# Attention followed by a gated expert layer: the fourth batch's first tiles turned by transposing transfers

## The chip, the cores and the metric

The kernel runs on one core of a Trainium2 chip. The metric is the device time of one execution in microseconds (us); less is better. Five engines run their own instruction streams in order and meet by semaphores: TensorE (PE in the profile, with its weight loads shown apart as PEld), VectorE (DVE), ScalarE (ACT), GpSimd (POOL) and SyncE (SP, which here only issues transfers). SBUF is the working memory of 128 partitions, PSUM the memory that TensorE writes to.

## The reference

All arithmetic is float32. Four batches, eight heads, 576 positions, head size 64:

```python
scores = q @ k^T / 8 + bias[h, i, j]      # bias: a small network of log1p(|i-j|) / log1p(max(i,1))
attn   = softmax(scores, axis=-1)         # exp(s - max) / (sum + 1e-9)
o      = attn @ v                         # (4, 8, 576, 64)
x      = o.transpose(0, 2, 1, 3).reshape(4 * 576, 512)
out    = ((x @ w_a) * (x @ w_b)) @ w_out  # w_a, w_b: 512 x 1536, w_out: 1536 x 512
```

## The kernel before

**Tiles.** Heads are taken in pairs (four pairs a batch). A unit is a batch, a pair and a half `c`: for `c = 0` the positions 0 to 255 of both heads, in four tiles of 128 rows of scores (`A0, B0, A1, B1`; A and B are the heads), for `c = 1` the positions 256 to 575 in five tiles (`A2, B2, A3, B3` and `T`, the last 64 rows of both heads). All `c = 0` units of the four batches come first (16 tiles a batch, tiles 0 to 63), then all `c = 1` units (20 tiles a batch, tiles 64 to 143). `N0 = 16`, `NF = 12` is the first unit of the fourth batch, `NP = 4`.

**One tile.** `qk` (L452) multiplies queries and keys into a PSUM pair `qk` (two banks, 288 keys in each); there is one such pair, so the scores of the next tile wait until VectorE has read those of this one. `soft1` (L489): VectorE adds the bias tile and takes the row minimum (L496, `p<-qk,bias`, minimum `mn`), ScalarE makes the exponential and its sum (L501). `soft2` (L540), one tile later: GpSimd and VectorE make the reciprocal `rc` (L544, L545), and then one of two ways is taken.

- Tiles 0 to 63: GpSimd scales the tile (L550), TensorE turns it in five 128-column pieces into a PSUM pair `tp` (`turn`, L562), ScalarE copies it to SBUF. In the fourth batch that copy is rounded to 16 bits (L578) and VectorE subtracts it from the PSUM tile for the rest (L579), so that `pt` holds high and low halves.
- Tiles 64 to 143, `split_turn` (L525): GpSimd writes the scaled tile rounded to 16 bits into the first half of a source buffer `ph` (L530), VectorE the rest into the second half in two instructions of 64 and 512 columns (L532), and SP issues one transposing transfer of `ph` into `pt` (L538). There are two `ph` buffers.

`pv` (L585) multiplies the turned tile with the values; in the fourth batch's first units it takes 15 products of both heads (30 matmuls), in `c = 1` units 14 (28 matmuls). The result goes as 16-bit high and low halves to `x`, the input of the expert layer.

**The second batch's scores** (tiles 16 to 31) are plain float32 products over 64 rows: head A's queries and keys stand on partitions 0 to 63, head B's on 64 to 127, and both matmuls of a tile (one for each half of the keys) read the same 64 partitions. The first batch's tiles are taken in pairs (`qk_pair`, L474): there the matmuls of a pair alternate between the two halves of the partitions, into two PSUM pairs.

**The expert layer** (`moe_block`, L684) for 256 rows: 24 steps of 12 matmuls (L698, `ab`), then 12 steps of 6 matmuls of the second product (L747, `o`). `merge` (L774) interleaves its steps with the steps of attention by fixed shares, and TensorE's order is this program order (`manual_schedule`, L796); the order on the other engines is planned when the kernel is built. Each block belongs to a batch and half whose attention is done. After the last attention step TensorE works through the rest of the expert layer alone.

**Bias.** The bias of rows 256 to 575 is made while the fourth batch's first tiles run: 20 units, each of four rectified rows (L143 on VectorE, L147 on ScalarE; `nact` of the four are on ScalarE), 32-column matmuls into PSUM (L153), copies (L169, L172) and a write to DRAM. One set of four `h` tiles is there.

**Order around the change.** In `attn_steps` (L621) step `n` runs `soft1(n)`, the preparation of units that begin soon, `qk(n + 1)`, `pv` of a unit that ended, `turn(n - 2)` and `soft2(n - 1)`; bias tiles are loaded two tiles ahead. At step 65 the pool of `pt` is closed and opened anew for the `c = 1` shapes (L667).

Of the kernel before, what the change touches and what calls it, by code (L numbers as in the profile page):

```python
# [8 lines left out]
F32 = mybir.dt.float32  # L9
# [43 lines left out]
def attention_moe(ctx, tc, q0d, q1d, kd, vd, idn, wp, wa, wb, wo, lsw, lg, rl, out):  # L53
# [10 lines left out]
    xt, cpool, epool, xpool = [], [None], [None], [None]  # L64
# [304 lines left out]
    def load_unit(u):  # L369
        b, hp, c = UNITS[u]  # L370
        n = TOK + TAIL * c
        if u < 2 * NP:
            rk = epool[0].tile([128, S], F32, tag="rkf", name="rkf", bufs=NP) if u < NP else \
                att.tile([128, S], F32, tag="ks", name="rkf", bufs=2)
            rq = epool[0].tile([128, TOK], F32, tag="rqf", name="rqf", bufs=NP) if u < NP else \
                att.tile([128, TOK], F32, tag="qs", name="rqf", bufs=2)
# [148 lines left out]
    def split_turn(n, p, rc):  # L525
        u, t = TILES[n]
        if t == "A2":
            st["pt", u] = cpool[0].tile([128, 9, 640], F16, tag="pt", name="pt", bufs=2)
        ph = cpool[0].tile([128, 2 * S], F16, tag="ph", name="ph", bufs=2)
# [7 lines left out]
        o = {"A2": 0, "A3": 128, "T": 256, "B2": 384, "B3": 512}[t]  # L537
        nc.sync.dma_start_transpose(out=st["pt", u][:, :, o:o + 128], in_=ph)  # L538

    def soft2(n):  # L540
# [5 lines left out]
        if UNITS[u][2]:  # L546
            split_turn(n, p, rc)
            return
# [7 lines left out]
    def turn(n, pool):  # L556
# [13 lines left out]
        if u < NF:  # L570
            if t == "A0":
                st["pt", u] = cpool[0].tile([128, 5, 512], F32, tag="pt", name="ptw", bufs=2)
            nc.scalar.copy(st["pt", u][:, :, o:o + 128], tp)
            return
        if t == "A0":
            st["pt", u] = cpool[0].tile([128, 10, 512], F16, tag="pt", name="pt", bufs=2)
        dst = st["pt", u][:, :, o:o + 128]
        nc.scalar.copy(dst[:, 0:5], tp)  # L578
        nc.vector.tensor_tensor(out=dst[:, 5:10], in0=tp, in1=dst[:, 0:5], op=ALU.subtract)  # L579
# [41 lines left out]
    def attn_steps():  # L621
        vgen = [None]
        for n in range(NT + 4):
# [11 lines left out]
            for ahead, un in ((a, TILES[n + a][0]) for a in (6, 4, 3, 1) if n + a < NT and FIRST[TILES[n + a][0]] == n + a):  # L635
# [11 lines left out]
                else:  # L647
# [20 lines left out]
            if n >= 2 and n - 2 < B * N0:  # L668
# [6 lines left out]
            elif N0 + 3 <= n < B * N0 + 3 and TILES[n - 3][0] != TILES[n - 2][0]:  # L675
# [123 lines left out]
    LEADS = [3] + [4] * 3 + [8] * 4  # L799
# [98 lines left out]
    n2, n3 = steps(2)[1], 2 * ((ends[3] - ends[2]) * 2 // 3)  # L898
# [4 lines left out]
    with tc.tile_pool(name="bg2", bufs=1, reuse_waits="tile") as bg:  # L903
# [71 lines left out]
```

## Time and profile before

| | us |
|---|---|
| median of three runs | 784.29 (778.23 to 787.6) |
| the profiled execution | 783.58 |
| its span, first to last instruction | 781.7 |
| TensorE busy | 724.0 (93%) |
| VectorE busy | 508.7 (65%) |
| ScalarE busy | 454.3 (58%) |
| GpSimd busy | 328.4 (42%) |
| mean granted TensorE clock | 0.985 |

A row of the profile names a line of the kernel, an engine, an operation and its tiles; "idle before" is the time in which the engine waited ahead of it, with what ended the wait. Matmuls are pipelined and their ends are modelled, so a busy TensorE is not one at its peak. The stages, by the start of the bias addition (L496) of their first tile: first batch to about 84 us, second to 159, third to 237, fourth to 337, the `c = 1` tiles to 650, and the expert layer alone to the end.

### The profile page before, as it was taken

The page shows a single profiled execution, that of the slowest core. Times are in us where ns is not written, and L with a number is a line of the kernel's source. Part 1 is how long each engine was busy: PE and PEld are TensorE (multiplying, and loading weights), DVE is VectorE, ACT ScalarE, POOL GpSimd, SP SyncE. Part 2 cuts the span into 40 slices and gives each one's busy share as a digit, 9 for nine tenths or more (in the row PEclk, how much of TensorE's full clock was granted, in tenths as well). Part 3 has the DMA queues.
Part 4 walks back from the last instruction along what each step waited for, and adds up shares of the span by engine and source line. Part 5 has one row for each costly group of instructions (what it writes and reads, how often), then busy time and mean ns, then how long its engine had stood idle before and what let it go on. Part 6 is the DMA issues. An engine that isn't in the chain of part 4 may idle for free.

```text
span 781.7 us, 15679 instructions
## 1 busy us (share of the span) xinstructions
PE 724.0 (93%) x5539; PEld 561.1 (72%) x5539; DVE 508.7 (65%) x1219; ACT 454.3 (58%) x1022; POOL 328.4 (42%) x493
## 2 busy tenths in 40 slices
PE   7778899999899999997888998998899999999998
PEld 1245566678777766786766777887787788888886
DVE  7677688679976788747878788877786762110100
ACT  6878787878866777744555455555554552421310
POOL 3347677856762233313444344534442453320200
PEclk9989999999999999999999999999999999999999
DMA  8998665688735555429988998999999863100001
GB/s 258 316 348 290 209 203 180 198 262 254 246 105 155 150 170 164 134 93 216 214 200 201 234 224 192 235 227 202 176 230 221 179 143 87 49 1 28 2 14 41
DMA packets 147699, 137.73 MB, mean 176 GB/s; under 512 B 101284, under 2 KB 105636, under 8 KB 147620
## 3 DMA queue, kind: packets, MB, share of 16 engines
q1 hardware_dynamic: 140464, 120.95, 58.9%
q10 hardware_dynamic: 5876, 10.93, 4.7%
q0 software_dynamic: 1280, 4.84, 1.8%
q8 instruction: 44, 0.72, 0.4%
q14 instruction: 35, 0.29, 0.1%
HBM read 95.91 MB, written 17.18 MB: 145 GB/s over the span
## 4 chain that ended last, share of the span: by engine, by line
PE 44%; DVE 16%; DMA 14%; issue 11%; ACT 7%; POOL 7%; SPq 0%; POOLq 0%; DVEq 0%; ACTq 0%
PE ab L698 16%; PE o L747 13%; DMA pt<-ph 10%; PE qk L468 4%; DVE p L496 4%; PE psta L153 3%; PE pv L599 3%; DVE ph L532 3%; POOL ph L530 3%; DMA bias<-bias_d 3%; ACT p L501 2%; PE tp L562 2%; DVE ks L400 1%; PE pr L828 1%; DVE wt L270 1%
## 5 line engine op out<-in xcount | busy, mean ns | idle before, releaser
L698 PEld LDWEIGHTS <-w16t 128*128 128x128 f16 x2592 | 249.3, 99 | 46.3 <-issue 13.8
L698 PE MATMUL ab<-x,w16t 128*128 128x256 f16 x2304 | 274.4, 275 | 0.6 <-DVE g L708 0.3
L501 ACT ACTIVATE p<-p,mn 128x576 f32<-128x576 f32 x144 | 111.7, 776 | 111.8 <-DVE mn L496 97.0
L496 DVE CUSTOM_DVE_ANT_0 p<-qk,bias 128x576 f32<-128x576 f32 x144 | 107.9, 751 | 30.7 <-PE tp L562 15.7
L747 PE MATMUL o<-wos,gh 128*128 128x512 f32 x384 | 121.0, 396 | 0.0
L723 POOL TENSOR_TENSOR gl<-g,gh 128x256 fp32r<-128x256 f32 x96 | 74.1, 772 | 93.1 <-ACT gh L722 90.9
L544 POOL TENSOR_SCALAR sm<-sm 128x1 f32<-128x1 f32 x144 | 41.9, 291 | 165.4 <-ACT p L501 161.0
L532 DVE SCALAR_TENSOR_TENSOR ph<-p,sm,ph 128x64 f16<-128x64 f32 (+1 forms) x160 | 85.4, 574 | 32.3 <-POOL ph L530 32.0
L530 POOL TENSOR_SCALAR ph<-p,sm 128x576 f16<-128x576 f32 x80 | 63.4, 793 | 73.5 <-DMA pt<-ph 50.7
L468 PE MATMUL qk<-ks,qs 128*128 128x288 f32 x384 | 74.0, 315 | 19.4 <-DVE mn L496 19.4
L708 DVE SCALAR_TENSOR_TENSOR g<-ab,wv,asb 128x256 f32<-128x256 f32 x84 | 40.2, 478 | 71.1 <-ACT asb L706 70.8
L747 PEld LDWEIGHTS o<-wos,gh 128*128 128x128 f32 x384 | 69.5, 188 | 16.2 <-issue 3.1
L468 PEld LDWEIGHTS qk<-ks,qs 128*128 128x128 f32 x384 | 56.2, 191 | 32.4 <-DVE mn L496 25.9
L747 PE MATMUL o<-wos,gl 128*128 128x512 f32 x192 | 75.0, 391 | 0.0
L550 POOL TENSOR_SCALAR p<-p,sm 128x576 f32<-128x576 f32 x64 | 59.2, 926 | 35.9 <-DVE sm L545 26.6
L722 ACT CAST gh<-g 128x256 fp32r<-128x256 f32 x96 | 38.5, 401 | 48.2 <-DVE g L708 48.0
L706 ACT ACTIVATE asb<-ab,wv 128x256 f32<-128x256 f32 x84 | 39.4, 469 | 34.2 <-PE ab L698 33.6
L562 PE MATMUL tp<-idn,p 128*128 128x128 f32 x320 | 48.4, 283 | 4.8 <-ACT ptf L567 4.5
L545 DVE RECIPROCAL sm<-sm 128x1 f32<-128x1 f32 x144 | 23.0, 159 | 41.2 <-POOL sm L544 38.5
L562 PEld LDWEIGHTS tp<-idn,p 128*128 128x128 f32 x320 | 37.6, 144 | 15.2 <-issue 5.4
L400 DVE TENSOR_TENSOR ks<-rk,ks 64x576 fp32r<-64x576 f32 x48 | 42.5, 885 | 3.8 <-ACT ks L399 2.0
L753 ACT COPY osb<-o 128x512 f32<-128x512 f32 x18 | 10.5, 585 | 57.8 <-PE o L747 42.0
(107 smaller groups left out, 1058.9 us busy)
## 6 DMA issues: line engine op xcount, KB each, us to landing
bias<-bias_d SPq DMA_DIRECT2D x128, 288.0 KB, 3.4
rv<-vd SPq DMA_DIRECT2D x32, 320.0 KB, 3.8
rk<-kd SPq DMA_DIRECT2D x24, 288.0 KB, 3.5
wraw<-wa SPq DMA_DIRECT2D x12, 512.0 KB, 6.7
wraw<-wb SPq DMA_DIRECT2D x12, 512.0 KB, 5.0
wraw<-wo SPq DMA_DIRECT2D x12, 512.0 KB, 4.1
bias_d<-bo ACTq DMA_DIRECT2D x20, 295.5 KB, 3.0
rq<-q1d SPq DMA_DIRECT2D x16, 320.0 KB, 4.4
```

The costliest lines, as they stand in the source:

```text
L400: nc.vector.tensor_tensor(out=ks[ol, j], in0=rk[sl], in1=ks[sl, j].bitcast(F32), op=ALU.subtract)
L468: nc.tensor.matmul(ps[:, hf, :HB], a, b[:, hf * HB:hf * HB + HB], start=(x == 0), stop=(x == len(prods) - 1))
L496: ttr = nc.vector.tensor_tensor_reduce(out=p.rearrange("p (a n) -> p a n", a=2), in0=ps[:, :, :HB], in1=bt.rearrange("p (a n) -> p a n", a=2),
L501: exps.append(nc.scalar.activation(p, p, AF.Exp, bias=mn, scale=-1.0, accum_out=sm))
L530: nc.gpsimd.tensor_scalar(out=ph[:, :S], in0=p, scalar1=rc, scalar2=1.0, op0=ALU.mult, op1=ALU.mult)
L532: ins = nc.vector.scalar_tensor_tensor(out=ph[:, o:o + c1 - c0], in0=p[:, c0:c1], scalar=rc, in1=ph[:, c0:c1], op0=ALU.mult, op1=ALU.subtract,
L544: nc.gpsimd.tensor_scalar(out=sm, in0=sm, scalar1=1e-9, scalar2=1.0 / (PS if u >= NF else 1.0), op0=ALU.add, op1=ALU.mult)
L550: nc.gpsimd.tensor_scalar(out=p, in0=p, scalar1=rc, scalar2=1.0, op0=ALU.mult, op1=ALU.mult)
L562: nc.tensor.transpose(tp[:, x, :], p[:, c0:c0 + 128], tab["idn"])
L698: nc.tensor.matmul(ab[:, j], w16[nm, f][:, pw, kk, :], xs[px][:, kk, :], start=(x % (3 * KC) == 0), stop=(x % (3 * KC) == 3 * KC - 1),)
L723: nc.gpsimd.tensor_tensor(out=gl, in0=g, in1=gh.bitcast(F32), op=ALU.subtract)
L747: nc.tensor.matmul(o, g[:, sl], wos[f][:, p], start=(f == 0 and x == 0), stop=(f == FC - 1 and x == 2))
```

## The change

Six edits:

1. Tiles 48 to 63 take `split_turn` instead of `turn`; their `pt` gets the layout of the `c = 1` tiles, and `pv` takes 14 products for them, one tile later than before (at step `n` for the unit that ended with tile `n - 4`). The values of a unit are prepared at its first tile instead of one tile ahead, from the fourth batch on.
2. A second pool `yp` of two `ph` buffers: all tiles up to 64 and the even ones after it use it, odd tiles after 64 use the old two. So the `c = 1` tiles have four buffers, the fourth batch's first tiles two.
3. From tile 51 on odd tiles' scores go to the PSUM pair `tp`, which no turn needs any more.
4. The second batch's keys are loaded with the first 288 keys of both heads on partitions 0 to 63 and the other 288 on 64 to 127, the queries (which stand twice in DRAM) whole on all 128; the two matmuls of a tile then read different halves of the partitions. Tiles 16 and 17 no longer go through `qk_pair`.
5. Of the four rectified rows of a bias unit, one or two in turn are on ScalarE (30 of 80 instead of 15 of 80).
6. Shares: the third expert block's first 24 steps run over 18 half-steps of attention instead of 20 and the bias stream ends one tile earlier; the block ends one tile later (`LEADS`); the pool `xp` is opened after the bias tiles are closed.

```diff
@@ load_unit
+            if u >= NP:
+                rk = att.tile([128, 2, HB], F32, tag="ks", name="rkf", bufs=2)
+                rq = att.tile([128, 2, TOK], F32, tag="qs", name="rqf", bufs=2)
+                with paced():
+                    for hf in range(2):
+                        src = kd[b, hp, :, hf * HB:hf * HB + HB].rearrange("(j d) n -> d j n", j=2)
+                        nc.sync.dma_start(out=rk[64 * hf:64 * hf + 64], in_=src)
+                    nc.sync.dma_start(out=rq, in_=q0d[b, hp])
+                st["raw", u] = rk, rq, None
+                return
...
-    def qk(n, pool):
+    def qk(n):
         u, t = TILES[n]
-        ps = pool.tile([128, 2, 512], F32, tag="qk", name="qk", bufs=1)
+        pool, tag = (tpp, "tp") if n > 3 * N0 + 2 and n % 2 else (qkp, "qk")
+        ps = pool.tile([128, 2, 512], F32, tag=tag, name="qk", bufs=1)
         q, k = st["qs", u], st["ks", u]
         if u < 2 * NP:
-            j = int(t[0] == "B")
-            sl, c0 = slice(64 * j, 64 * j + 64), 128 * int(t[1])
-            prods = [(q[sl, c0:c0 + 128], k[sl])]
+            j, c0 = int(t[0] == "B"), 128 * int(t[1])
+            for hf in range(2):
+                sl = slice(64 * hf, 64 * hf + 64)
+                nc.tensor.matmul(ps[:, hf, :HB], q[sl, j, c0:c0 + 128], k[sl, j, :], start=True, stop=True)
+            st["qk", n] = ps
+            return
@@ split_turn
-        if t == "A2":
-            st["pt", u] = cpool[0].tile([128, 9, 640], F16, tag="pt", name="pt", bufs=2)
-        ph = cpool[0].tile([128, 2 * S], F16, tag="ph", name="ph", bufs=2)
+        if t in ("A0", "A2"):
+            st["pt", u] = cpool[0].tile([128, 9, 512 + 128 * UNITS[u][2]], F16, tag="pt", name="pt", bufs=2)
+        pool = cpool[0] if n > B * N0 and n % 2 else ypool[0]
+        ph = pool.tile([128, 2 * S], F16, tag="ph", name="ph", bufs=2)
@@ soft2
-        if UNITS[u][2]:
+        if u >= NF:
             split_turn(n, p, rc)
@@ turn
-        if t == "A0":
-            st["pt", u] = cpool[0].tile([128, 10, 512], F16, tag="pt", name="pt", bufs=2)
-        dst = st["pt", u][:, :, o:o + 128]
-        nc.scalar.copy(dst[:, 0:5], tp)
-        nc.vector.tensor_tensor(out=dst[:, 5:10], in0=tp, in1=dst[:, 0:5], op=ALU.subtract)
...
-    LAST = [[(0, 4, 9)], []]
@@ attn_steps
-            for ahead, un in ((a, TILES[n + a][0]) for a in (6, 4, 3, 1) if ...
+            for ahead, un in ((a, TILES[n + a][0]) for a in (6, 4, 3, 1, 0) if ...
-                else:
+                elif ahead == int(un < NF):
-            if n + 1 < N0 + 2:
+            if n + 1 < N0:
                 if n % 2:
                     qk_pair(n + 1)
-            if n >= B * N0 + 4 and (n - 3 >= NT or TILES[n - 4][0] != TILES[n - 3][0]):
+            if n >= 3 * N0 + 4 and (n - 3 >= NT or TILES[n - 4][0] != TILES[n - 3][0]):
                 pv(TILES[n - 4][0], pvp)
-            if n >= 2 and n - 2 < B * N0:
+            if n >= 2 and n - 2 < 3 * N0:
                 turn(n - 2, tpp)
@@ main
-    LEADS = [3] + [4] * 3 + [8] * 4
+    LEADS = [3, 4, 4, 5] + [8] * 4
-                lambda g: bg.tile(...), u, un, int(un % 4 != 3)
+                lambda g: bg.tile(...), u, un, 1 + un % 2
-    n2, n3 = steps(2)[1], 2 * ((ends[3] - ends[2]) * 2 // 3)
+    n2, n3 = steps(2)[1], 2 * (B * N0 - 3 - ends[2])
+        ypool[0] = ctx.enter_context(tc.tile_pool(name="yp", bufs=1, side="right", reuse_waits="tile"))
```

## Rows read from the trace of the kernel before

**Rows 1.** The page's busy time: engine, busy us, share of the span, instructions.

```profile
PE 724.0 (93%) x5539; PEld 561.1 (72%) x5539; DVE 508.7 (65%) x1219; ACT 454.3 (58%) x1022; POOL 328.4 (42%) x493
```

**Rows 2.** Stretches by stage: busy us of each engine, granted clock, DMA share, GB/s.

```profile
core 0: us, PE busy (x) PEld busy (x) DVE busy (x) ACT busy (x) POOL busy (x), PEclk, DMA share, GB/s
84.00:159.00 75.00, 70.77 (x501) 48.76 (x501) 56.95 (x146) 59.49 (x133) 57.03 (x70) 1.00 0.63 195
237.00:337.00 100.00, 99.66 (x824) 71.34 (x822) 73.71 (x162) 72.28 (x155) 27.31 (x46) 1.00 0.51 148
337.00:650.00 313.00, 287.05 (x2269) 240.79 (x2268) 237.41 (x571) 167.61 (x390) 129.72 (x224) 0.98 0.89 200
650.00:782.00 132.00, 127.63 (x879) 108.76 (x877) 14.06 (x32) 30.18 (x69) 24.77 (x35) 1.00 0.09 29
```

**Rows 3.** The page's chain that ended last, shares of the span by line.

```profile
PE ab L698 16%; PE o L747 13%; DMA pt<-ph 10%; PE qk L468 4%; DVE p L496 4%; PE psta L153 3%; PE pv L599 3%; DVE ph L532 3%; POOL ph L530 3%; DMA bias<-bias_d 3%; ACT p L501 2%; PE tp L562 2%; DVE ks L400 1%; PE pr L828 1%; DVE wt L270 1%
```

**Rows 4.** Groups of TensorE from 337 to 650 us: busy us, mean ns, idle before.

```profile
L468 PE MATMUL qk<-ks,qs 128*128 128x288 f32 x252 | 48.3, 314 | 14.4 <-DVE mn L496 14.4
...
L468 PE MATMUL qk<-ks,qt 128*128 128x288 f32 x128 | 22.5, 322 | 11.6 <-DVE mn L496 11.6
```

**Rows 5.** The page's costliest groups, those of the source buffers.

```profile
L532 DVE SCALAR_TENSOR_TENSOR ph<-p,sm,ph 128x64 f16<-128x64 f32 (+1 forms) x160 | 85.4, 574 | 32.3 <-POOL ph L530 32.0
L530 POOL TENSOR_SCALAR ph<-p,sm 128x576 f16<-128x576 f32 x80 | 63.4, 793 | 73.5 <-DMA pt<-ph 50.7
```

**Rows 6.** Start of the `c = 1` tiles: start us, us, engine, line, operation [idle before].

```profile
354.72 0.74 POOL L530 TENSOR_SCALAR ph<-p,sm 128x576 f16<-128x576 f32 x1 [6.90 <-DMA pt<-ph]
...
355.21 2.26 PE L468 MATMUL qk<-ks,qt 128*128 128x288 f32 x8 [2.94 <-DVE mn L496]
```

**Rows 7.** Groups of TensorE from 237 to 337 us.

```profile
L562 PE MATMUL tp<-idn,p 128*128 128x128 f32 x83 | 11.8, 272 | 0.0
```

**Rows 8.** Timeline of TensorE in the fourth batch's first tiles.

```profile
302.45 1.92 PE L153 MATMUL psta<-h,w2s 128*32 128x512 f32 x8
...
304.94 0.71 PE L562 MATMUL tp<-idn,p 128*128 128x128 f32 x5
...
305.58 1.95 PE L599 MATMUL pv<-pt,vs 128*64 128x256 f16 x30
...
308.87 1.10 PE L153 MATMUL psta<-h,w2s 128*32 128x288 f32 x16
```

**Rows 9.** Groups of VectorE, 237 to 337 us and, for L532, 337 to 650.

```profile
L579 DVE TENSOR_TENSOR pt<-tp,pt 128x640 f16<-128x640 f32 x13 | 10.7, 822 | 0.8 <-ACT pt L578 0.6
...
L532 DVE SCALAR_TENSOR_TENSOR ph<-p,sm,ph 128x512 f16<-128x512 f32 x79 | 58.7, 744 | 0.0
L532 DVE SCALAR_TENSOR_TENSOR ph<-p,sm,ph 128x64 f16<-128x64 f32 x79 | 32.0, 405 | 32.3 <-POOL ph L530 32.0
```

**Rows 10.** Groups of ScalarE and GpSimd from 237 to 337 us.

```profile
L578 ACT CAST pt<-tp 128x640 f16<-128x640 f32 x14 | 9.7, 693 | 8.6 <-PE tp L562 8.4
...
L550 POOL TENSOR_SCALAR p<-p,sm 128x576 f32<-128x576 f32 x16 | 14.2, 886 | 9.0 <-DVE sm L545 6.5 <-PE psta L153 1.7 <-PE ab L698 0.8
```

**Rows 11.** The tile `h`, instructions by line: ns shortest/median/longest, first and last start.

```profile
L143 DVE TENSOR_SCALAR h<-u,lgs x65: 367/440/1007, 238.5 to 320.3; 128x320 f32<-128x320 f32 x7, 128x304 f32<-128x304 f32 x6, 128x384 f32<-128x384 f32 x4, 128x448 f32<-128x448 f32 x4
L147 ACT ACTIVATE h<-u,lgs x15: 546/640/767, 238.9 to 316.8; 128x304 f32<-128x304 f32 x2, 128x320 f32<-128x320 f32 x1, 128x336 f32<-128x336 f32 x1, 128x352 f32<-128x352 f32 x1
```

**Rows 12.** The tile `ph`: the transposing transfers, issue time, and time to landing.

```profile
L538 SPq DMA_TRANSPOSE pt<-ph x80: 1241/1378/2420, 351.2 to 651.7; - x80
...
DMA to landing us min/median/max: 3.2/3.8/5.9
```

**Rows 13.** Timeline of TensorE: first batch's paired scores, second batch's scores.

```profile
57.41 1.62 PE L482 MATMUL qk<-rkf,rqf 64*128 64x288 f32 x8
...
117.70 1.23 PE L468 MATMUL qk<-rkf,rqf 64*128 64x288 f32 x4
```

**Rows 14.** Stretches of 15 us in the `c = 1` tiles, columns as in rows 2.

```profile
355.00:370.00 15.00, 14.47 (x108) 12.35 (x108) 10.44 (x28) 7.65 (x17) 6.22 (x12) 0.89 1.13 232
370.00:385.00 15.00, 11.66 (x96) 9.68 (x97) 12.81 (x30) 8.28 (x20) 7.33 (x12) 0.89 0.86 192
```

**Rows 15.** The page's DMA issues: transfers, KB each, us to landing.

```profile
bias<-bias_d SPq DMA_DIRECT2D x128, 288.0 KB, 3.4
```

More of the change, by code (lines that the diff above doesn't have):

```diff
@@ L63, in attention_moe @@
     winv = cst.tile([128, FC, 2], F32, name="winv")
-    xt, cpool, epool, xpool = [], [None], [None], [None]
+    xt, cpool, epool, xpool, ypool = [], [None], [None], [None], [None]
     vsc = []
@@ L372, in load_unit @@
         if u < 2 * NP:
[L373 to L376, printed above, removed]
+            if u >= NP:
[8 more added lines that the diff above has]
+                return
+            rk = epool[0].tile([128, S], F32, tag="rkf", name="rkf", bufs=NP)
+            rq = epool[0].tile([128, TOK], F32, tag="rqf", name="rqf", bufs=NP)
             with paced():
@@ L536, in split_turn @@
         pns.append(ins)
-        o = {"A2": 0, "A3": 128, "T": 256, "B2": 384, "B3": 512}[t]
+        o = {"A0": 0, "A1": 128, "B0": 256, "B1": 384, "A2": 0, "A3": 128, "T": 256, "B2": 384, "B3": 512}[t]
         nc.sync.dma_start_transpose(out=st["pt", u][:, :, o:o + 128], in_=ph)
@@ L569, in turn @@
         o = {"A0": 0, "A1": 128, "B0": 256, "B1": 384}[t]
-        if u < NF:
-            if t == "A0":
-                st["pt", u] = cpool[0].tile([128, 5, 512], F32, tag="pt", name="ptw", bufs=2)
-            nc.scalar.copy(st["pt", u][:, :, o:o + 128], tp)
-            return
         if t == "A0":
-            st["pt", u] = cpool[0].tile([128, 10, 512], F16, tag="pt", name="pt", bufs=2)
-        dst = st["pt", u][:, :, o:o + 128]
-        nc.scalar.copy(dst[:, 0:5], tp)
-        nc.vector.tensor_tensor(out=dst[:, 5:10], in0=tp, in1=dst[:, 0:5], op=ALU.subtract)
+            st["pt", u] = cpool[0].tile([128, 5, 512], F32, tag="pt", name="ptw", bufs=2)
+        nc.scalar.copy(st["pt", u][:, :, o:o + 128], tp)
     TERMS = [(0, x, x) for x in range(4)] + [(1, x, x) for x in range(4)]
     TERMS += [(0, x, 5 + x) for x in range(4)] + [(0, 4, 4), (1, 4, 4)]
-    LAST = [[(0, 4, 9)], []]
     def pv(u, pool):
@@ L593, in pv @@
         else:
-            rows = [slice(64 if vb == 4 and not c else 0, 128) for _, vb, _ in TERMS + LAST[c]]
-            prods = [(vs[sl, part, vb], pt[sl, pb]) for (part, vb, pb), sl in zip(TERMS + LAST[c], rows)]
+            prods = [(vs[:, part, vb], pt[:, pb]) for part, vb, pb in TERMS]
         for x, (v, p) in enumerate(prods):
@@ L634, in attn_steps @@
                 next(stream[0], None)
-            for ahead, un in ((a, TILES[n + a][0]) for a in (6, 4, 3, 1) if n + a < NT and FIRST[TILES[n + a][0]] == n + a):
+            for ahead, un in ((a, TILES[n + a][0]) for a in (6, 4, 3, 1, 0) if n + a < NT and FIRST[TILES[n + a][0]] == n + a):
                 if un < NP:
@@ L662, in attn_steps @@
             elif n + 1 < NT:
-                qk(n + 1, qkp)
-            if n >= B * N0 + 4 and (n - 3 >= NT or TILES[n - 4][0] != TILES[n - 3][0]):
+                qk(n + 1)
+            if n >= 3 * N0 + 4 and (n - 3 >= NT or TILES[n - 4][0] != TILES[n - 3][0]):
                 pv(TILES[n - 4][0], pvp)
@@ L674, in attn_steps @@
                     pv_first(n - 3, pvp)
-            elif N0 + 3 <= n < B * N0 + 3 and TILES[n - 3][0] != TILES[n - 2][0]:
+            elif N0 + 3 <= n < 3 * N0 + 3 and TILES[n - 3][0] != TILES[n - 2][0]:
                 pv(TILES[n - 3][0], pvp)
@@ L884, in rows @@
             return bias_relu(
-                lambda g: bg.tile([128, S], F32, tag=f"h{g}", name=f"h{g}", bufs=1), u, un, int(un % 4 != 3)
+                lambda g: bg.tile([128, S], F32, tag=f"h{g}", name=f"h{g}", bufs=1), u, un, 1 + un % 2
             )
@@ L908, in attention_moe @@
         stream[1] = [2 * first + 2 * nst * i // nb for i in range(nb)]
+        ypool[0] = ctx.enter_context(tc.tile_pool(name="yp", bufs=1, side="right", reuse_waits="tile"))
         merge((main, 2 * FC - 22 + GS + 1), (asteps, n2 - n2 * 5 // 8))
-        xpool[0] = ctx.enter_context(tc.tile_pool(name="xp", bufs=1, side="right", reuse_waits="tile"))
         main = moe_main(2, 0, mps)
@@ L913, in attention_moe @@
         run(stream[0])
+    xpool[0] = ctx.enter_context(tc.tile_pool(name="xp", bufs=1, side="right", reuse_waits="tile"))
     merge((main, GS + 1), (asteps, steps(3)[1] - n3))
```

## Prediction

> **What bounds the kernel now.** I began with the busy shares of the page [rows 1]: TensorE is busy for 724 of 781.7 us, so at most 58 us of its time is idle, and a gain must come from work that leaves TensorE or from its idle time. The mean says nothing of place, so next I cut the span by stage [rows 2]. Three things are to be seen there. The fourth batch's first tiles (237 to 337 us) have TensorE busy for 99.66 of 100 us, with VectorE and ScalarE at 74% and 72%: TensorE bounds them. The `c = 1` tiles (337 to 650) have TensorE at 287 of 313 us, 26 us idle, and DMA at 0.89. From 650 us on TensorE is alone with the expert layer; 132 us that the change does not touch. Third, the waits in the `c = 1` tiles: all 26.0 us of TensorE's idle time (14.4 + 11.6) stand ahead of a score product that waits for VectorE's row minimum of the tile before [rows 4], that is for the one PSUM pair. Behind that VectorE waited 32.0 us for GpSimd's half of `ph`, and GpSimd 50.7 us for a transposing transfer to give back a source buffer [rows 5]; the chain that ended last holds 10% of those transfers [rows 3]. So the loop there is buffer, GpSimd, VectorE, PSUM pair, TensorE.
>
> **The fourth batch's first tiles.** Edit 1 takes 16 x 5 turns from TensorE. 83 of them were busy for 11.8 us [rows 7], 0.142 us each, so 80 are 11.4 us; a tile's five take 0.71 us in the timeline [rows 8], which gives the same. Two of 30 `pv` matmuls go in four units: 1.95 / 30 x 2 x 4 = 0.5 us [rows 8]. Together 11.9 us of a stage in which TensorE never rests.
>
> What takes over must fit. VectorE loses 16 x 0.822 and gains 16 x (0.744 + 0.405) [rows 9], and edit 5 takes 15 rectified rows of 0.440 from it [rows 11]: 73.7 - 13.2 + 18.4 - 6.6 = 72.3 us. ScalarE loses 16 x 0.693 [rows 10] and gains 15 x 0.640 [rows 11]: 72.3 - 11.1 + 9.6 = 70.8 us. GpSimd changes 0.886 [rows 10] for 0.793 [rows 5]. In a stage of some 90 us that is 80% for either busy engine: hidden, but not deeply. SP issues 16 transfers of 1.38 us [rows 12], 22 us, and behind each stands a bias load that lands in 3.4 us [rows 15] and was issued two tiles, some 11 us, ahead: hidden. Two source buffers: GpSimd 0.79, VectorE 1.15 and landing 3.8 (longest 5.9) [rows 5, 9, 12] are 5.7 to 7.8 us a buffer, 2.9 to 3.9 us a tile, under the 5.6 us of a tile: hidden. DMA: this stage moves 14.8 MB in 51 us of share, 3.45 us a MB; the `c = 1` tiles move 62.6 MB in 279 [rows 2]. Taking 80 transfers of 0.295 MB (two halves of 128 x 576 x 2 bytes) out of these and pricing the other 39 MB at 3.45 leaves an estimate of 1.8 us a transfer. 51 + 16 x 1.8 = 80 us of 90: it fits, and a stretch of 1.13 [rows 14] says that 1.0 is no wall. Values prepared at the unit's first tile and `pv` one tile later cost nothing: a unit's `pv` comes seven tiles after its first.
>
> I take 9 of the 11.9 us. The reason is in [rows 8]: eight bias products lasted 1.92 us where sixteen took 1.10 elsewhere, so some of TensorE's busy time is a wait for the one set of `h`, which the turns now cover. Bounds: 0 to 11.9.
>
> By the same rows TensorE loaded weights for 71% of this stage, against 82% in the part after 650 us where it is alone [rows 2]. The Trainium skill (Perfetto Trace Analysis, Identifying the Most-Contended Engine) says that matmul busy time is a poor measure of how near TensorE is to its limit and that the share of LDWEIGHTS is a better one. By that rule 1 - 71/82 = 13 us of the stage are slack, and the turns were partly filling it; the gain would be near 3 us, not 9. That is rival 3.
>
> **The `c = 1` tiles.** Edits 2 and 3 meet the loop at both ends. With four buffers one is asked for every fourth tile: 5.7 to 7.8 us a buffer over four tiles are at most 2 us a tile, under the 3.9 us of a tile (313 / 80), so most of the 50.7 us goes. With two PSUM pairs the scores of tile n + 1 wait for the minimum of tile n - 1, 3.9 us earlier than now, and the waits seen at one place were 2.94 us [rows 6]. What is late next is VectorE: 237 us of work in 313, plus the handshake that stays with every tile (GpSimd's 0.79 between the reciprocal and L532). I leave 10 of the 26 us to that: gain 16. Bounds: 0 (VectorE's waits on GpSimd are all handshake) and 26, with 5 more from the clock: the stage has a mean of 0.98 and stretches of 0.89 right after long idle times [rows 14], so 313 x 0.02 = 6 us of clock are lost now, and no more than that can come back.
>
> One stall stays. At step 65 the first transfer of the new shapes must wait for the last `pv` of the old ones, and now this comes one tile later; behind it on SP stand bias loads. Before, GpSimd stood 6.90 us there and TensorE 2.94 [rows 6]. With four buffers GpSimd no longer stands, but a bias tile behind two issues of 1.38 lands 2 x 1.38 + 3.4 = 6.2 us after the `pv` [rows 12, 15]; with two expert steps and a score product as cover I see about 3 us, as now. No gain is booked there.
>
> **The second batch's scores.** The two matmuls on one half of the partitions take 1.23 us a tile; eight that alternate between halves serve two tiles in 1.62 [rows 13], 0.81 each: 0.42 x 16 = 6.7 us. TensorE is 94% busy there, but VectorE, ScalarE and GpSimd are at 76 to 79% [rows 2] with the weight preparation between them. I take 3. Bounds: 6.7, and a loss of 2: tiles 16 and 17 lose their second PSUM pair for one tile, and four units load 128 KB more of queries, 0.7 us each at 195 GB/s, under a DMA share of 0.63 and some six tiles ahead.
>
> **Sum.** The profiled execution took 783.58 us: 781.7 of span and 1.9 around it; the median of the runs is 0.7 us higher, which I ignore. 783.6 - 9 - 16 - 3 = 755.6, so **756 us**.
>
> **Rivals.**
> 1. *The `c = 1` tiles hardly move.* The order of work on VectorE and GpSimd is planned anew, and the handshake (32.0 us, rows 5) simply takes the place of the buffer wait: 3 us there. For it: VectorE waits more for GpSimd than TensorE waits at all. Against: 50.7 us of GpSimd's waits are the buffers'. 783.6 - 9 - 3 - 3 = 769. Chance 0.20.
> 2. *All of it comes.* 11.9 + 26 + 5 + 3 = 46: 738. For it: idle time and clock hang together. Against: VectorE would be busy for 237 of 282 us, 84%, where it is 76% now. Chance 0.10.
> 3. *TensorE has slack in the fourth batch* (3 there, 16, 3): 762. For it: the 1.92 us of [rows 8]. Against: TensorE's idle time there is 0.34 us in all [rows 2]. Chance 0.14.
> 4. *No difference.* The fourth batch's tiles meet VectorE and ScalarE at 80%, and the handshake eats the rest: 2 + 3 + 0 gives 779. Chance 0.09.
> 5. *Slower: the two source buffers of the fourth batch.* GpSimd's queue also splits the expert layer's products (`gl`), so when it stands at L530 TensorE's second product stands too. The point from which it decides: a landing of more than 2 x 6.2 - 1.94 = 10.5 us, since a tile there takes 6.2 us. With the bias writes on the same DMA engines and landings of, say, 14 us, a tile takes (1.94 + 14) / 2 = 8.0 us: 16 x 1.8 = 29 us more; with nothing gained elsewhere 812. Against: the longest landing at a share of 0.89 was 5.9 us [rows 12]. Chance 0.05.
>
> That the halves of the partitions do not overlap (3 us less) lies within the forecast's own range.
>
> **How the numbers follow.** The forecast has the remaining 0.42, with a range of its own of 748 to 765 (4 to 11.9 in the fourth batch, 10 to 22 in the `c = 1` tiles, 0 to 6.7 in the second batch, not all at one end). The range that should hold the time 8 times in 10 takes in rivals 1 and 3 and half of 2 and leaves out 4, 5 and the rest of 2: 743 to 774. About 1%, 8 us, is what a measurement of this kernel can tell from no change: faster than 776 are the forecast and rivals 1 to 3, 0.86; rival 4 is 0.09; rival 5 is 0.05.
>
> **What would show it.** After the change, tiles 48 to 63 should take 88 to 93 us instead of 100 with TensorE still above 97% busy; if TensorE shows waits for `h` or `ph` there, rival 3 or 5 holds. In the `c = 1` tiles GpSimd's wait for transfers should fall from 50.7 to under 15 us and TensorE's wait for the minimum from 26 to about 10; if the first falls and the second does not, rival 1 holds and VectorE's wait for GpSimd will have grown. Score products of the second batch should stand at about 0.8 us a tile. The prediction is wrong if the stage after 650 us changes length, or if the new plan of the engines moves time into the first 84 us.

## The result

The changed kernel takes 760.31 us (median of 4 runs, 758.25 to 765.74) against 785.34 for the kernel before, run in the same rounds (778.23 to 787.6): a ratio of 0.9707, 95% interval 0.9626 to 0.9788. The forecast was 756 with 743 to 774. The profiled execution took 758.25 us with a span of 756.4, where before it was 783.58 and 781.7.

I cut both spans at the start of the bias addition of tiles 0, 16, 32, 48 and 64, and then at the first matmul of the `o` steps that run when the last tile's bias addition comes (648.01 us before, 622.73 after; 886 matmuls start from there on in both, so it is the same place in TensorE's order):

| stretch | before, us | after, us | difference | forecast |
|---|---|---|---|---|
| up to tile 0 | 36.8 | 36.5 | -0.3 | 0 |
| tiles 0 to 15 | 46.9 | 44.9 | -2.0 | 0 |
| tiles 16 to 31 (second batch) | 75.4 | 75.4 | 0 | -3 |
| tiles 32 to 47 | 78.1 | 78.6 | +0.5 | 0 |
| tiles 48 to 63 (fourth batch) | 99.2 | 97.0 | -2.2 | -9 |
| tile 64 to those `o` steps (`c = 1`) | 311.5 | 290.3 | -21.2 | -16 |
| from there to the end | 133.7 | 133.7 | 0 | 0 |

So the total is near the forecast, and its parts are not: the `c = 1` tiles gave 5.2 us more than was booked and the stretches booked at 0 gave 1.8, while the fourth and the second batch gave 9.8 less. That these errors cancel is luck. The 2.0 us of tiles 0 to 15 are no more than executions differ there: tile 16 began between 80.1 and 85.6 us in the kernels told of below, at 80.1 in the one that leaves the first two batches as they were before. The last stretch begins, in the timeline of after (the second row is the last tile's bias addition, at 646.88 before):

```profile
622.73 0.72 PE L751 MATMUL o<-wos,gh 128*128 128x512 f32 x2
...
625.72 0.74 DVE L508 CUSTOM_DVE_ANT_0 p<-qk,bias 128x576 f32<-128x576 f32 x1
```

The last tile's addition now falls 3.0 us behind that matmul, where it fell 1.1 us ahead of it. Whoever cuts at the last tile sees 4.1 us less in the rest of the expert layer; cut at TensorE's own order, that stage has not changed.

### The profile page after: what moved, and what is told of

It reads as the page before. It is cut to its first block, busy times and chain, and to the rows that moved or that the text cites. A ratio compares the mean times of both kernels' runs of the same rounds, so it can differ in the third digit from the quotient of the medians.

```text
span 756.4 us, 15529 instructions
## 1 busy us (share of the span) xinstructions
PE 703.1 (93%) x5451; PEld 541.8 (72%) x5451; DVE 506.8 (67%) x1220; ACT 448.5 (59%) x1021; POOL 338.3 (45%) x493
## 4 chain that ended last, share of the span: by engine, by line
PE 33%; DVE 22%; issue 16%; ACT 11%; POOL 9%; DMA 7%; SPq 0%; DVEq 0%; POOLq 0%; ACTq 0%
PE ab L702 12%; PE o L751 10%; DVE p L508 5%; DVE ph L545 4%; POOL ph L543 4%; DMA bias<-bias_d 4%; ACT p L513 3%; PE psta L153 3%; POOL gl L727 2%; DVE ks L408 2%; PE pv L603 2%; DMA pt<-ph 2%; PE qk L480 2%; DVE wt L270 1%; DVE qs L427 1%
## 5 line engine op out<-in xcount | busy, mean ns | idle before, releaser
L702 PEld LDWEIGHTS <-w16t 128*128 128x128 f16 x2592 | 247.5, 98 | 47.7 <-issue 15.8
L702 PE MATMUL ab<-x,w16t 128*128 128x256 f16 x2304 | 271.1, 274 | 4.1 <-DVE g L712 2.0
L727 POOL TENSOR_TENSOR gl<-g,gh 128x256 fp32r<-128x256 f32 x96 | 79.4, 827 | 93.6 <-ACT gh L726 91.9
L751 PE MATMUL o<-wos,gh 128*128 128x512 f32 x384 | 120.8, 395 | 0.0
L545 DVE SCALAR_TENSOR_TENSOR ph<-p,sm,ph 128x64 f16<-128x64 f32 x192 | 100.3, 562 | 22.8 <-POOL ph L543 22.1
L508 DVE CUSTOM_DVE_ANT_0 p<-qk,bias 128x576 f32<-128x576 f32 x144 | 107.3, 748 | 12.0 <-PE tp L575 4.1
L543 POOL TENSOR_SCALAR ph<-p,sm 128x576 f16<-128x576 f32 x96 | 82.4, 858 | 49.4 <-DVE sm L558 37.4
L480 PE MATMUL qk<-ks,qs 128*128 128x288 f32 x384 | 73.0, 312 | 13.8 <-DVE mn L508 13.8
L751 PEld LDWEIGHTS o<-wos,gh 128*128 128x128 f32 x384 | 69.4, 188 | 16.3 <-issue 3.3
L480 PEld LDWEIGHTS qk<-ks,qs 128*128 128x128 f32 x384 | 55.8, 188 | 27.4 <-DVE mn L508 18.7
L751 PE MATMUL o<-wos,gl 128*128 128x512 f32 x192 | 75.0, 391 | 0.0
L563 POOL TENSOR_SCALAR p<-p,sm 128x576 f32<-128x576 f32 x48 | 44.5, 927 | 26.6 <-DVE sm L558 18.3
L408 DVE TENSOR_TENSOR ks<-rk,ks 64x576 fp32r<-64x576 f32 x48 | 45.8, 954 | 5.7 <-ACT ks L407 4.1
L751 PEld LDWEIGHTS o<-wos,gl 128*128 128x128 f32 x192 | 36.0, 188 | 7.9
L575 PE MATMUL tp<-idn,p 128*128 128x128 f32 x240 | 36.0, 281 | 5.0 <-ACT ptf L580 3.6
L603 PE MATMUL pv<-pt,vs 128*64 128x320 f16 (+1 forms) x560 | 40.4, 295 | 0.0
```

The source lines that it names most:

```text
L408: nc.vector.tensor_tensor(out=ks[ol, j], in0=rk[sl], in1=ks[sl, j].bitcast(F32), op=ALU.subtract)
L480: nc.tensor.matmul(ps[:, hf, :HB], a, b[:, hf * HB:hf * HB + HB], start=(x == 0), stop=(x == len(prods) - 1))
L508: ttr = nc.vector.tensor_tensor_reduce(out=p.rearrange("p (a n) -> p a n", a=2), in0=ps[:, :, :HB], in1=bt.rearrange("p (a n) -> p a n", a=2),
L543: nc.gpsimd.tensor_scalar(out=ph[:, :S], in0=p, scalar1=rc, scalar2=1.0, op0=ALU.mult, op1=ALU.mult)
L545: ins = nc.vector.scalar_tensor_tensor(out=ph[:, o:o + c1 - c0], in0=p[:, c0:c1], scalar=rc, in1=ph[:, c0:c1], op0=ALU.mult, op1=ALU.subtract,
L563: nc.gpsimd.tensor_scalar(out=p, in0=p, scalar1=rc, scalar2=1.0, op0=ALU.mult, op1=ALU.mult)
```

## The profile after

Lines are shifted: L508 is the bias addition and minimum (before L496), L543 and L545 the two halves of `ph` (L530, L532), L551 its transfer (L538), L480 and L469 score products (L468), L603 `pv` (L599), L575 the turn (L562), L702 and L751 the expert layer (L698, L747).

The page of the changed kernel: busy time [rows 1], the chain that ended last [rows 3], and the groups of the source buffers [rows 5].

```profile
PE 703.1 (93%) x5451; PEld 541.8 (72%) x5451; DVE 506.8 (67%) x1220; ACT 448.5 (59%) x1021; POOL 338.3 (45%) x493
...
PE ab L702 12%; PE o L751 10%; DVE p L508 5%; DVE ph L545 4%; POOL ph L543 4%; DMA bias<-bias_d 4%; ACT p L513 3%; PE psta L153 3%; POOL gl L727 2%; DVE ks L408 2%; PE pv L603 2%; DMA pt<-ph 2%; PE qk L480 2%; DVE wt L270 1%; DVE qs L427 1%
...
L545 DVE SCALAR_TENSOR_TENSOR ph<-p,sm,ph 128x64 f16<-128x64 f32 x192 | 100.3, 562 | 22.8 <-POOL ph L543 22.1
...
L543 POOL TENSOR_SCALAR ph<-p,sm 128x576 f16<-128x576 f32 x96 | 82.4, 858 | 49.4 <-DVE sm L558 37.4
```

The transposing transfers fall from 10% to 2% of the chain. GpSimd now waits for VectorE's reciprocal rather than for a buffer, and VectorE's wait for GpSimd is 22.1 us, although 96 tiles take this way instead of 80. The waits of the `c = 1` tiles (who waits for whom, us, times, longest):

```profile
PE qk L480 <- DVE mn L508: 8.9, 11, 1.4
...
POOL ph L543 <- DMA pt<-ph: 11.4, 2, 6.6
```

TensorE's wait for the minimum falls from 26.0 to 8.9 us [rows 4], GpSimd's for transfers from 50.7 to 11.4 [rows 5]. The stretches, columns as in [rows 2], first those of after: the fourth batch's first tiles, and the `c = 1` tiles up to those `o` steps.

```profile
235.30:332.40 97.10, 93.59 (x731) 62.21 (x732) 69.06 (x159) 70.82 (x154) 26.25 (x43) 1.00 0.76 183
...
332.40:622.70 290.30, 277.95 (x2268) 235.70 (x2262) 238.58 (x567) 160.59 (x382) 137.72 (x222) 1.00 0.96 219
```

The same two stretches in the kernel before, cut alike:

```profile
237.20:336.50 99.30, 98.96 (x820) 70.76 (x819) 73.23 (x161) 71.80 (x154) 27.31 (x46) 1.00 0.51 149
...
336.50:648.00 311.50, 285.55 (x2262) 239.52 (x2261) 237.44 (x569) 166.42 (x385) 128.50 (x221) 0.98 0.89 200
```

In the `c = 1` tiles TensorE's idle time falls from 26.0 to 12.3 us (length less busy) and its busy time by 7.6 us with the same expert and score work. In the fourth batch its busy time falls by 5.4 us and its idle time rises from 0.3 to 3.5. The groups of TensorE there (busy us, mean ns, idle before) show how; first after, then before:

```profile
L153 PE MATMUL psta<-h,w2s 128*32 128x288 f32 (+17 forms) x192 | 24.1, 473 | 3.1 <-ACT h L147 1.4 <-ACT osb L757 0.8 <-ACT gh L726 0.7
...
L603 PE MATMUL pv<-pt,vs 128*64 128x256 f16 x72 | 4.5, 275 | 0.0
...
L575 PE MATMUL tp<-idn,p 128*128 128x128 f32 x11 | 1.7, 272 | 0.0
```

```profile
L153 PE MATMUL psta<-h,w2s 128*32 128x288 f32 (+17 forms) x192 | 20.5, 473 | 0.0
...
L562 PE MATMUL tp<-idn,p 128*128 128x128 f32 x81 | 11.6, 272 | 0.0
L599 PE MATMUL pv<-pt,vs 128*64 128x256 f16 (+1 forms) x90 | 5.8, 275 | 0.0
```

9.9 us of turns and 1.3 of `pv` are gone. The same 192 bias products now take 3.6 us more, and 3.1 us of idle time stands ahead of them. At one such place:

```profile
266.32 1.68 PE L153 MATMUL psta<-h,w2s 128*32 128x384 f32 x8
...
267.17 0.14 PEld L153 LDWEIGHTS psta<-h,w2s 128*32 128x32 f32 x2 [0.70 <-ACT h L147]
```

The weight load in the middle of eight products waits for ScalarE's second rectified row: that is edit 5.

## Experiments

Times are medians with the ratio to the kernel before in the same rounds. "From tile 64" is from the start of that tile's bias addition to the end in the profiled execution: 445.2 us before, 424.0 after. Six kernels with the same code from there on (after, `d1`, `d4`, `c1`, `c2`, `c3`) lie between 422.8 and 426.0.

### One or two PSUM pairs, two or four source buffers

Edit 3 undone (`e1`):

```diff
-        pool, tag = (tpp, "tp") if n > 3 * N0 + 2 and n % 2 else (qkp, "qk")
+        pool, tag = qkp, "qk"
```

> The changed kernel with all scores on the one PSUM pair again (edit 3 undone); four source buffers stay. The c = 1 tiles (start of tile 64 to start of tile 143) took 310 us before and 293 after. Theory (both ends of the loop matter): GpSimd's wait for transfers stays small (about 11 us), TensorE's wait for the minimum stays near 20 us, the tiles take 300 to 306, the run 767 to 774. Rival A (the buffers alone did it): 293 and 760. Rival B (the PSUM pair alone did it): 308 or more and 775 or more.

Edit 2 undone (`e2`):

```diff
-        pool = cpool[0] if n > B * N0 and n % 2 else ypool[0]
+        pool = ypool[0]
```

> The changed kernel with two source buffers for all tiles (edit 2 undone); the second PSUM pair stays. Theory (both ends matter): GpSimd waits 40 us or more for transfers again, TensorE's wait moves to other places but stays at 10 to 20 us, the c = 1 tiles take 300 to 306 us, the run 767 to 774. Rival A (the buffers alone did it): 308 or more and 775 or more. Rival B (the PSUM pair alone did it): 293 and 760.

Both undone (`e3`):

> The changed kernel with edits 2 and 3 both undone. Theory: the c = 1 tiles are back at 308 to 312 us and the run at 774 to 780, so that these two edits are worth 14 to 20 us and all others together 5 to 10. Rival C (what helped the c = 1 tiles is something else, such as the changed shares or a new plan of the engines): 300 or less and under 768.

| | time, us | ratio | from tile 64 | TensorE's wait for the minimum |
|---|---|---|---|---|
| after | 760.31 | 0.9707 [0.9626, 0.9788] | 424.0 | 8.9 |
| one pair | 773.71 | 0.985 [0.9812, 0.9888] | 434.9 | 17.0 |
| two buffers | 786.93 | 1.0024 [0.9992, 1.0056] | 450.8 | 24.8 |
| one pair, two buffers | 792.58 | 1.0097 [1.0064, 1.013] | 457.0 | 33.2 |

From the start of tile 64 to that of tile 143, the measure of the expectations, the three take 301.4, 320.1 and 323.5 us. The theory's 300 to 306 held for one pair and missed for two buffers, and with both undone 308 to 312 were expected.

Four buffers give 22.1 us with one pair and 26.8 with two; the second pair gives 6.2 us with two buffers and 10.9 with four. Together they give 33.0. Each seems to be worth more with the other, but the 4.7 us on which this rests are little more than the 3.2 by which the same code differs between executions. With two buffers the page reads:

```profile
L543 POOL TENSOR_SCALAR ph<-p,sm 128x576 f16<-128x576 f32 x96 | 82.1, 855 | 89.8 <-DMA pt<-ph 61.3
L545 DVE SCALAR_TENSOR_TENSOR ph<-p,sm,ph 128x64 f16<-128x64 f32 x192 | 101.2, 566 | 51.9 <-POOL ph L543 51.3
```

So the buffer bounds the loop, as read from [rows 5], and VectorE's wait for GpSimd goes with it: rival 1 falls. But with both undone the kernel is slower than before by 11.8 us from tile 64 on, and in that part only the edits costed at nothing are left: the later values, and the shares.

### The later values

The last kernel with the values of a `c = 1` unit prepared one tile ahead again, but for the first unit (`f1`):

```diff
-                elif ahead == int(un < NF):
+                elif ahead == int(un < NF or un > B * NP):
```

> The kernel with edits 2 and 3 undone, which took 323.5 us for the c = 1 tiles where the kernel before took 310.4, with one more thing as before: the values of the c = 1 units are prepared one tile ahead of the unit again. Theory V (that step, 1.2 us of VectorE ahead of a half of ph at the unit's first tile, is what made those tiles slower): 309 to 313 us, the run 778 to 782. Rival (the shares of the expert layer or the place of the first stall did it): 320 or more, the run 789 or more.

784.52 us, ratio 1.0011 [0.9978, 1.0044], above the 778 to 782 expected; tiles 64 to 143 take 312.3 us, within theory V's 309 to 313. From tile 64 on it is 447.2 instead of 457.0, 2.0 from the kernel before. So nearly all of the loss is the later values: 9.8 us in the profiled executions, 6.7 by the two ratios. In the kernel with one pair and two buffers, at a unit's first tile:

```profile
518.12 0.74 POOL L543 TENSOR_SCALAR ph<-p,sm 128x576 f16<-128x576 f32 x1 [4.38 <-DMA pt<-ph]
518.90 0.95 DVE L545 SCALAR_TENSOR_TENSOR ph<-p,sm,ph 128x64 f16<-128x64 f32 x2 [3.70 <-POOL ph L543]
...
522.36 1.23 DVE L440 SCALAR_TENSOR_TENSOR vs<-rv,vs,vs 128x640 f16<-128x640 f32 x1 [0.28 <-ACT vs L439]
523.52 0.94 DVE L545 SCALAR_TENSOR_TENSOR ph<-p,sm,ph 128x64 f16<-128x64 f32 x2
...
525.18 0.79 PE L480 MATMUL qk<-ks,qs 128*128 128x288 f32 x4 [0.97 <-DVE mn L508]
```

VectorE splits the values between two tiles' `ph`, and the scores after it wait for the minimum. That this is how the 9.8 us arise is read from this place alone.

### Edits 2 and 3 alone, on the kernel before

The kernel before, values early, turns in the fourth batch, with four buffers and the second score pair for the `c = 1` tiles only (`g1`):

```diff
+        pool, tag = (tpp, "tp") if n > B * N0 + 2 and n % 2 else (qkp, "qk")
...
-        ph = cpool[0].tile([128, 2 * S], F16, tag="ph", name="ph", bufs=2)
+        pool = cpool[0] if n % 2 else ypool[0]
+        ph = pool.tile([128, 2 * S], F16, tag="ph", name="ph", bufs=2)
...
```

> The kernel before with edits 2 and 3 for the c = 1 tiles alone: four source buffers and two PSUM pairs from tile 64 on; the fourth batch's first tiles are turned by TensorE as before. Theory (edit 1 gives 2 us and no more, and edits 2 and 3 the rest): tiles 48 to 63 take 99 us, the c = 1 tiles 288 to 296, the run 758 to 766. If edit 1 matters beyond its stage (no turn at the seam, an earlier second pair): 768 or more. If the later values cost something in the change: 755 or less.

757.61 us, ratio 0.9678 [0.9623, 0.9734]; from tile 64 on 419.3, 25.9 less than before; tiles 48 to 63 take 99.2, as before. GpSimd no longer waits for a transfer there:

```profile
L532 POOL TENSOR_SCALAR ph<-p,sm 128x576 f16<-128x576 f32 x80 | 68.3, 855 | 30.7 <-DVE sm L547 30.5
```

These two edits hold the whole measured gain; edits 1, 4, 5 and 6 together add nothing that can be told from zero. Edit 6 has no run of its own.

### The rectified rows

Edit 5 undone (`d1`):

```diff
-                ..., u, un, 1 + un % 2
+                ..., u, un, int(un % 4 != 3)
```

> The changed kernel with the rectified rows shared as before (edit 5 undone: 15 of 80 on ScalarE). Tiles 48 to 63 took 99.2 us before and 97.0 after, where the removed turns alone should have given some 89; after, TensorE's bias products waited 5.6 us for rows on ScalarE. Theory W (edit 5 put the second ScalarE row in TensorE's way): 91 to 94 us there, the run 754 to 757. Rival H (one set of h serialises the stream whoever makes the rows, or VectorE is next): 97 to 100 us, the run 760 to 763.

756.65 us, ratio 0.9681 [0.9613, 0.9748]; tiles 48 to 63 take 94.5 us instead of 97.0, half a microsecond above theory W's range. The eight kernels with edit 5 take 97.0 to 98.6 there. Another way to relieve VectorE, one row of each bias unit on GpSimd and one on ScalarE (`d4`):

```diff
-                nc.vector.tensor_scalar(
+                (nc.gpsimd if g == 0 and un >= NU0 else nc.vector).tensor_scalar(
...
-                ..., u, un, 1 + un % 2
+                ..., u, un, 1
```

> The changed kernel with, of the four rectified rows of a unit, one on GpSimd, one on ScalarE and two on VectorE. Theory W: a row on an engine that is 28% busy comes as early as the other three, 90 to 94 us for tiles 48 to 63, the run 753 to 757. Rival H: 96 to 99 us, 759 to 762. Slower than 100 us there if a row on GpSimd waits behind its exponential sums.

759.03 us, ratio 0.9699 [0.9644, 0.9755]; tiles 48 to 63 take 98.9. These are rival H's numbers, but in its trace the bias products wait for the new row:

```profile
PEld psta L153 <- POOL h L143: 7.3, 10, 1.9
...
PE psta L153 <- POOL h L143: 4.5, 6, 1.6
```

The row moved to GpSimd comes late here, as the second one on ScalarE did. With the old rows TensorE still waits there, now for ScalarE's copies of the bias:

```profile
PE ab L702 <- ACT bo L172: 2.4, 3, 1.0
PE psta L153 <- ACT osb L757: 0.8, 1, 0.8
...
PE psta L153 <- ACT h L147: 0.5, 1, 0.5
```

### Old rows and early values; bias products in the turn's banks

The changed kernel with the old rows and the early values (`h1`):

> The changed kernel with two things as before: the values of the c = 1 units prepared one tile ahead, and 15 of 80 rectified rows on ScalarE. The first alone was worth 11.2 us of the c = 1 tiles with two buffers and one pair, the second 2.5 us of tiles 48 to 63. If they add up here: tiles 48 to 63 at 94 to 96 us, the c = 1 tiles at 285 to 288 us instead of 293, the run 747 to 752. If four buffers already hide the later values: 292 to 294 and 755 to 758.

758.58 us, ratio 0.9661 [0.9603, 0.9719]. Tiles 48 to 63 take 95.4, tiles 64 to 143 288.7, between the two ranges expected, and from tile 64 on it is 421.5. With `g1` and `h2` (419.3, 419.7), the kernels with early values beside four buffers lie between 419.3 and 421.5, against 422.8 to 426.0 with late ones: about 4 us, less than half of the cost with two buffers. Against `d1` (423.4), which differs from `h1` in nothing else, it is 1.9, and part of that is clock: `d1` was granted the lower of TensorE's two levels once there, at 355.6 us, `h1` never. The total does not show it: the first 32 tiles of this execution, in which its code is that of after, took 126.7 us, the longest of nine executions of the same program there (the shortest took 119.2). The granted clock was 0.89 in these tiles, against 0.97 in after and 1.00 in `d1`.

The same with the bias products in the PSUM pair that the turns left, and with the second score pair from tile 63 on only, to see whether the ring of PSUM tiles that they share with the expert layer holds the stage (`h2`):

```diff
-        pool, tag = (tpp, "tp") if n > 3 * N0 + 2 and n % 2 else (qkp, "qk")
+        pool, tag = (tpp, "tp") if n > B * N0 - 2 and n % 2 else (qkp, "qk")
...
-            ... mps.tile([128, 1, 2 * TOK], F32, tag="ab", name="psta", bufs=3) ...
+            ... tpp.tile([128, 2, 512], F32, tag="tp", name="psta", bufs=1) ...
```

> The kernel of the run above with the bias products in the PSUM pair that the turns left free, and the second score pair from tile 63 on only. Theory P (with the turns gone TensorE comes early to the three-deep PSUM ring that it shares with the bias products, whose banks ScalarE frees by its copies): tiles 48 to 63 at 88 to 92 us, the run 4 to 6 us under the run above. Rival H (one set of h serialises the stream): 94 to 96 us, no change. Slower there if the one score pair makes TensorE wait for the minimum again: 97 or more.

760.84 us, ratio 0.9714 [0.9672, 0.9755]; tiles 48 to 63 take 100.1, and the products wait 6.8 us for the copies; TensorE never waits for the minimum there. The one pair makes the products wait, so this does not settle what a larger ring would do. A second set of `h` tiles and four `bo` tiles were not tried.

### The second batch's scores

Edit 4 undone, but for the pairing of tiles 16 and 17 (`c1`):

```diff
-                sl = slice(64 * hf, 64 * hf + 64)
-                nc.tensor.matmul(ps[:, hf, :HB], q[sl, j, c0:c0 + 128], k[sl, j, :], ...)
+                nc.tensor.matmul(ps[:, hf, :HB], q[sl, c0:c0 + 128], k[sl, hf * HB:hf * HB + HB], ...)
```

> The changed kernel with the second batch's scores as before (edit 4 undone but for the pairing of tiles 16 and 17). Tiles 16 to 31 took 75.4 us before and after. Theory D (VectorE with the weight preparation bounds this stage, TensorE's saved time became a wait for the minimum): 75 to 76 us again, the run within 3 us of 760, TensorE's wait for the minimum there falls from 5.1 to about 2 us. Rival E (edit 4 was worth 3 us or more and something else in the change ate it): 78.5 us or more and 763 or more.

762.19 us, ratio 0.971 [0.9678, 0.9743]; 1.9 us above the changed kernel, within the spread of the runs. Tiles 16 to 31 take 78.7 us; nine kernels with the edit take 74.8 to 77.9 there, the two others without it 75.4 (before) and 79.3 (`g1`), so the times tell little; TensorE's wait for the minimum is 1.8 us there, as theory D said. To see whether VectorE hides the edit, two kernels without one of VectorE's instructions of the weight preparation (the weights lose their three lowest bits), with edit 4 (`c2`) and without (`c3`):

```diff
-        nc.vector.scalar_tensor_tensor(
-            out=u, in0=lo, scalar=29, in1=u, op0=ALU.logical_shift_right, op1=ALU.bitwise_or
-        )
```

> The changed kernel without the VectorE instruction that puts the three lowest bits into the converted weights (the weights lose those bits): 36 instructions of 0.7 us go, 13 of them, some 9 us, between the starts of tiles 16 and 32, which took 75.4 us. Theory D (VectorE with the weight preparation bounds this stage): 67 to 71 us there, and TensorE's wait for the minimum falls from 5.1 us to 3 or less. Rival E (TensorE or the loads bound it): 73 to 75.5 us.

> The same lighter weight conversion, and the second batch's scores on one half of the partitions again (edit 4 undone but for the pairing). Theory D: with VectorE relieved TensorE is the next bound there, so edit 4 now shows: tiles 16 to 31 take 3 to 6 us longer than with the lighter conversion alone. Rival: within 1.5 us of it, as edit 4 was within its spread without the relief.

753.34 us (751.91 to 754.85) with the edit and 755.97 (755.18 to 756.49) without: 2.6 us, and the runs do not overlap. Tiles 16 to 31 take 70.7 and 74.1 us, and TensorE waits 3.4 us for the minimum with the edit (theory D: 3 or less) and not at all without. So VectorE's load in that batch holds more than the scores do, and once it is lighter the edit is worth about the 3 us that the forecast gave it.

## Why the prediction was right, and where it was not

**The loop of the `c = 1` tiles: right in mechanism, too small.** The chain buffer, GpSimd, VectorE, PSUM pair, TensorE was read rightly, and each of the two edits breaks it where the prediction said. 16 us were forecast, 21.2 measured. The working left 10 us of TensorE's waits for the minimum, and 8.9 are left; but new waits of 3.4 us stand ahead of the expert layer's products, so the idle time falls by 13.6 us. The other 7.6 are busy time, which the forecast booked at nothing and kept as "5 more from the clock": the granted clock was 0.89 between 355 and 385 us before and 0.99 from there on, and is 1.00 now. 30 x 0.11 + 263 x 0.01 give an estimate of 5.9 us. These are means between the two levels of 2.4 and 1.2 GHz. Before, the lower level was granted four times in these tiles, at 355.2 (the seam, [rows 6]), 372.2, 403.0 and 539.5 us, each time within 1.4 us of the end of a wait for the minimum of 2.3 to 2.9 us (a fifth wait, of 2.1 us up to 421.7, was not followed by it); now the longest such wait there is 1.4 us, and the lower level is not granted. So rival 2 (all of it, with the clock) was half true. The mis-sized terms are the clock, booked at nothing, and the 10 us left standing: edits 2 and 3 alone leave 5.8 us of that wait and gave 25.9 (`g1`), and the later values take some of it back in the change.

**The fourth batch's first tiles: the step that failed is "I take 9 of the 11.9 us".** 2.2 came, and rival 3 had given 3. The work left TensorE as counted (9.9 + 1.3 of 11.9 us by the groups). The reason named for taking less than all, that the turns cover a wait for `h`, was right; what failed is its size, 2.9 us booked where 9.7 were lost. The turns had filled the places in which the bias products wait for their rows; without them the products last 3.6 us longer and TensorE is idle 3.2 us more. 2.5 us of the loss are edit 5's: without it (`d1`) the stage is 4.7 us shorter than before. The rest is overlap, since busy times of groups that run beside each other add up to more than the stretch; that part is not shown by a run. TensorE was to be above 97% busy there; it is at 96% (93.59 of 97.1). The sign was named beforehand: waits for `h`. Rival 3's sum, 762, is nearer to the measured time than the forecast.

The share of weight loads, 71% against 82% with TensorE alone, pointed to this, and the busy share of 99.66% did not. The Trainium skill (Perfetto Trace Analysis, Identifying the Most-Contended Engine) holds the first to be the better measure; the trace agrees in the direction, with 2.2 us measured (4.7 without edit 5) against an estimate of 3 by it and 9 by the busy share. The 3 does not follow from the 13 us of slack, which would have hidden all 11.9; the prediction shows no working for it. In the stretch of after the share is 64% (62.21 of 97.1).

**Edit 5 and the later values were costed at nothing, and were not free.** The cover named for edit 5 was ScalarE's average of 80%; but ScalarE's row is one of four that a bias unit needs, with one set of `h`, so its delay is passed on to TensorE: 2.5 us (`d1`). For the values the cover was that `pv` comes seven tiles later. That is true for TensorE and says nothing of VectorE, which splits the values in the middle of the loop that bounds the stage: up to some 4 us with four buffers and 7 to 10 with two. That this splitting is the way it costs was read at one place.

**The second batch's scores: right per tile, not in the sum.** A product takes 0.76 us instead of 1.23 [rows 13], as forecast, and the wait ahead of it has grown:

```profile
120.41 0.76 PE L469 MATMUL qk<-rkf,rqf 64*128 64x288 f32 x4 [1.35 <-DVE mn L508]
...
PE qk L469 <- DVE mn L508: 5.1, 3, 2.5
```

It was 1.8 us before. The 3 us are there only when VectorE has less to do.

**The seam: the wait stayed, and cost nothing.** I expected GpSimd not to stand there and TensorE to stand for 3 us. It is the other way round: GpSimd waited 6.63 us where it had waited 6.90 [rows 6], and TensorE ran on, with a score product and a `pv` without a wait ahead of either:

```profile
341.90 0.74 POOL L543 TENSOR_SCALAR ph<-p,sm 128x576 f16<-128x576 f32 x1 [6.63 <-DMA pt<-ph]
...
344.50 1.24 PE L480 MATMUL qk<-ks,qt 128*128 128x288 f32 x8
345.67 1.72 PE L603 MATMUL pv<-pt,vs 128*64 128x256 f16 x28
```

In `g1`, where TensorE turns the fourth batch and all four buffers are free when the `c = 1` tiles begin, GpSimd does not stand there. So the prediction was right for four free buffers; in the change the fourth batch's last tiles still hold two of them.

Rivals 4 and 5 did not happen: the landings that the view counts (74 of 96) lay between 3.2 and 6.6 us. By their semaphores in the trace the longest of the others are those of tiles 62 and 63, at the seam, 7.5 and 8.5 us after issue. All are below the 10.5 from which two buffers would have held the fourth batch. What holds that stage after edit 1 (one set of `h`, ScalarE's copies or the ring of PSUM tiles) stays open.

## What to carry to other kernels

Work taken from an engine that is busy all the time is worth its duration only if the rest of its work is ready earlier; look for matmuls that last longer in one place than in another, for here they held waits that the removed work had been hiding. Where a loop runs over several engines, cost every instruction that a change moves into it on each of them, also one whose result is needed much later. And look at both ends of such a loop: more buffers at one end and a second one at the other gave 22.1 and 6.2 us apart and 33.0 together in the changed kernel, and 25.9 together in the kernel before, where the values come early.

## What the runs showed of the hardware

The transfers nearly kept their median landing time while the DMA engines were fuller. With the share of DMA in the `c = 1` tiles at 0.96 instead of 0.89 (single stretches of 15 us reached 1.10 after and 1.13 before), the transposing transfers that the view counts land in a median of 4.0 us instead of 3.8, the longest in 6.6 instead of 5.9; SP needs longer to issue one, 1467 ns instead of 1378 [rows 12].

```profile
370.00:385.00 15.00, 13.89 (x128) 11.55 (x128) 12.52 (x34) 10.53 (x26) 9.27 (x15) 1.00 1.10 240
...
L551 SPq DMA_TRANSPOSE pt<-ph x96: 1242/1467/2999, 240.2 to 630.5; - x96
...
DMA to landing us min/median/max: 3.2/4.0/6.6
```

Two float32 products of 64 rows and 288 columns (four matmul instructions in the trace) that read different halves of the partitions take 0.76 us together, and 1.23 on the same half [rows 13].
